# Eight quarter places of 4 KB in place of two whole places of 16 KB for x, the first keys and values, the last raw weights and the sums of w_in

## The chip, the core and the metric

The kernel runs on one core of one Trainium2 chip. The metric is the device time in microseconds of one execution, the median over the runs shown. A matmul is issued by TensorE (PE; PEld is its weight load), element-wise work runs on VectorE (DVE), ScalarE (ACT) and GpSimd (POOL), and SyncE (SP) issues almost all DMA transfers.

## What is computed

The reference is an attention with keys and values that are averaged over groups of 8 positions, followed by a two-layer network with a sigmoid gate:

```python
# q, k, v: [8, 8, 576, 64]; w_in: [512, 2048]; w_out: [2048, 512]
k_p = k.reshape(B, H, 72, 8, D).mean(axis=3)
v_p = v.reshape(B, H, 72, 8, D).mean(axis=3)
scores = np.matmul(q, k_p.transpose(0, 1, 3, 2)) / np.sqrt(D)
attn = softmax(scores)
x = np.matmul(attn, v_p).transpose(0, 2, 1, 3).reshape(B * S, H * D)   # [4608, 512]
h = x @ w_in
g = h * (1.0 / (1.0 + np.exp(-1.702 * h)))
out = g @ w_out
```

## The kernel before, in words

The 4608 tokens are worked through in nine chunks of 512. Chunks 0 to 7 are the first 512 tokens of each batch; the 64 tokens that every batch leaves over are gathered through DRAM into chunk 8. For each chunk the attention gives x, transposed, as a rounded part and a rest; every matmul of the network is then made of three products (rounded by rounded, rest by rounded, rounded by rest).

- **Attention of batch b.** Four matmuls (L961 to L964) form one column block `pav{b}_{piece}_{j}` in a PSUM bank of the two-bank ring `ps_a`. ACT or DVE writes its rounded part into x (L989), DVE the rest (L992), and for batches from 2 on the whole value is copied too (L1001). The transposed attention weights `apt` (L883) use the same two banks. So the third user of this ring waits until the DVE has read the first.
- **Chunks 0 and 1** go through `dense`: h = x @ w_in (L1220 to L1222), the gate on ACT (L1237, L1242), its rest on POOL (L1250), and o += g @ w_out (L1262 to L1264).
- **Chunks 2 to 8** go through `pair`: two 128-row blocks of w_in at once by a scheme with seven products instead of eight (L1424), collected in two PSUM banks `ha` and `hb` of the two-bank ring `ps_h`; DVE or ACT copies the bank `ha` out (L1439), DVE adds the bank `hb` (L1446), and the outputs are L1624 to L1626. The scheme needs sums and differences of blocks of x and of w_in. The latter are formed once, by `fold(p)` for p = 0 to 7 (L1307 the sums, L1332 the rounded part, L1335 the rest), kept in the buffer `stage` and written to DRAM (`wd{p}_{k}`, L1297, k = 1 and 2 from `stage`). Each later chunk reads them back (L1357).
- **Where x lies.** The pool `xpool` has two places of 16 KB per partition under one tag `x`. They go, in this order, to `kv0` (pooled inputs of batch 0), `x0`, the last three raw weight blocks (`raws`), `x1`, `stage`, and then the operands of chunks 2 to 8. A place is handed on when the last use of all of it is over. So chunk 2's x takes the place of `stage`: its first write on ACT waits for all the last DMA writes of `stage` (folds 6 and 7).
- **Loads of keys and values.** From batch 1 on, `kv{b}_{u}_False` (k) and `kv{b}_{u}_True` (v) take turns in a single place, and DVE sums each over the pooling windows (`red`, L539) before the next is loaded.
- **Order.** The program first lists every task with an estimated length and a due time. `Plan.order` then runs a list schedule over engines, places and banks and fixes a single order for each of the engines and for the DMA issues on SP. Hence a change of places changes the order of many instructions that it doesn't name. At run time every engine takes its instructions strictly in that order and waits by semaphore.

Of the kernel before, what the change touches and what calls it, by code (L numbers as in the profile page):

```python
# [10 lines left out]
F32 = mybir.dt.float32  # L11
F32R = mybir.dt.float32r
U32 = mybir.dt.uint32
# [5 lines left out]
P = 128  # L19
# [237 lines left out]
def attention_moe_kernel(ctx: ExitStack, tc: tile.TileContext, q, k, v, w_in, w_out, out):  # L257
# [110 lines left out]

    x_bufs = {}

    def x_buf(c):
        if c not in x_bufs:
            x_bufs[c] = buf(xpool, [P, 2, NJ, CHUNK], F32R, "x", f"x{c}", fifo=True)
        return x_bufs[c]


# [46 lines left out]

    def x_op(c, name):
        if c not in x_ops:
            xb = buf(xpool, [P, 2, NJ, CHUNK], F32R, "x", f"x{c}", fifo=True)
            at = [(xb, lambda t, k=k: t[:, :, k]) for k in range(NJ)]
            at += [(home(2 * i, [P, 2, 512], F32R, f"xs{c}_{i}"), lambda t: t) for i in X_PLACES[(c - FROM) % 2]]
            x_ops[c] = {n: Op(b, n, view) for n, (b, view) in zip(XOPS, at)}
        return x_ops[c][name]  # L430

    def x_whole(c, name):
# [439 lines left out]
    def weigh(b, piece, m, main, tail):  # L872
# [50 lines left out]
        for j in range(NJ):  # L923
# [41 lines left out]

            kh, jj = divmod(j, 2)
            if b < FROM:
                parts_of, whole = (x,), None
            else:

                block, whole = (("11", "t1"), ("21", "t4"), (None, "t3"), ("22", "t2"))[2 * piece + kh]
                block, whole = x_op(b, block) if block else None, x_whole(b, whole)
                parts_of = [o.of for o in (block, whole) if o]
# [6 lines left out]
                mode="f32r",  # L980
            )
            if b < FROM:
                hk, lk = [(x, (0, piece, j))], [(x, (1, piece, j))]
                hv, lv = (lambda j=j, r=r: x()[:, r, j, cols] for r in range(2))
            elif block:
                hk, lk = (block.refs(r, (jj,)) for r in range(2))
                hv, lv = (lambda jj=jj, r=r, block=block: block(r, jj) for r in range(2))
# [79 lines left out]
    def home(i, shape, dtype, name):  # L1067
        return Buf(home_ring(i), lambda: const.tile(shape, dtype, tag=f"w{i}", name=name), name)

    def fetch_weights(i):  # L1070
        f, m, c0, n = parts[i]
        if i + GAP < 2 * NF:
            raw = home(i + GAP, [P, n, 2], U32, f"raw{i}")
        else:

            if not last_raws:
                last_raws.append(buf(xpool, [P, 2, 512, 2], U32, "x", "raws", fifo=True))
            kk = i + GAP - 2 * NF
            sl = ((kk + 1) // 2, slice((kk // 2) * 256, (kk // 2) * 256 + n))
            raw = Part(last_raws[0], kk, lambda t: t[:, sl[0], sl[1]])  # L1080
        rows = slice(f * P, (f + 1) * P)
        src = w_out[rows, c0 : c0 + n].unsqueeze(1) if m else w_in[:, rows].rearrange("(j p) c -> p j c", p=P)
        words = src.bitcast(U32).rearrange("p j (c w) -> p j c w", w=2)
        dma(
            P * n * 8,
            lambda: nc.sync.dma_start(
                out=raw().rearrange("p (j c) w -> p j c w", j=words.shape[1]), in_=words
            ),
            writes=[ref(raw)],
        )  # L1090
        raws[i] = raw
# [115 lines left out]
    def dense(c, o0, n, fs, acc, due):  # L1207
# [6 lines left out]
        for i, f in enumerate(fs):  # L1214
            for j in range(NJ):

                def products(i=i, f=f, j=j):
                    w, o = homes[0, f]().rearrange("p r (j c) -> p r j c", j=NJ), h()[:, i]
                    xs = xb()[:, :, :, o0 : o0 + n]
                    nc.tensor.matmul(o, lhsT=w[:, 0, j], rhs=xs[:, 0, j], start=j == 0, stop=False)  # L1220
                    nc.tensor.matmul(o, lhsT=w[:, 1, j], rhs=xs[:, 0, j], start=False, stop=False)  # L1221
                    nc.tensor.matmul(o, lhsT=w[:, 0, j], rhs=xs[:, 1, j], start=False, stop=j == NJ - 1)  # L1222

                pe(
                    3 * (0.4167 * n + 13.5),
                    products,
                    [homes[0, f]] + [(xb, (r, hf, j)) for r in range(2) for hf in halves],
                    [h],
                    mode="f32r",
                )  # L1230
# [58 lines left out]
    def fold(p):  # L1289

        pair_of = [homes[0, 2 * p + i] for i in range(2)]
        d1, d2 = (Sums(stage, 2 * (p % 2) + i, lambda t, k=2 * (p % 2) + i: t[:, :, k]) for i in range(2))

        def leave(k, reads, view):
            dma(
# [216 lines left out]

    def first_batch():
        m = Batch()
        kv = buf(xpool, [P, 2, NU, NP, 512], F32, "x", "kv0", fifo=True)
        m.k, m.v = ([Part(kv, (i, u), lambda t, i=i, u=u: t[:, i, u]) for u in range(NU)] for i in range(2))
        m.tl = home(2 * NF - 4, [P, 512], F32, "tl0")
        whole = []
        tiles = PIECES[0][1] + PIECES[1][1]
        places = [home(2 * NF - 1 - i, [P, 2, H, D], F32, f"q0_{i}") for i in range(3)]  # L1520

        def fetch_q_tile(i):
            s0, ns = tiles[i]
            part = Part(places[i // 2], i % 2, lambda t: t[:ns, i % 2])
            dma(
                ns * H * D * 4,
                lambda: nc.sync.dma_start(out=part(), in_=q[0, :, s0 : s0 + ns].rearrange("h s d -> s h d")),
                writes=[ref(part)],
                run=256,
            )  # L1530
            whole.append(part)

        todo = {
            "k0": lambda: fetch_main(0, 0, k, m.k[0]),
            "k1": lambda: fetch_main(0, 1, k, m.k[1]),
            "v0": lambda: fetch_main(0, 0, v, m.v[0]),
            "v1": lambda: fetch_main(0, 1, v, m.v[1]),
            "t": lambda: fetch_last(0, m.tl),
            "w": lambda: fetch_weights(len(raws)),
            "q": lambda: fetch_q_tile(len(whole)),  # L1540
        }
        for n, what in enumerate("k0 k1 t q q v0 v1 w w w w w q q q w w".split()):
            plan.due = -100.0 + n
            todo[what]()
        return m, whole[:2], whole[2:]
# [13 lines left out]
    for b in range(1, B):  # L1559
        m = Batch()  # L1560
        m.k = m.v = m.tl = None
        start = FIRST + STEP * (NF + LAG) + ROUND * (b - 2) if b > 1 else 90.0
        plan.start = start - 15
        plan.due = start
        sum_keys(b, m)
        plan.due = start + 5
        held = scores(b, 0, m)
        sum_values(b, m)
        plan.due = start + 15
        weigh(b, 0, m, *held)  # L1570
        plan.due = start + 20
        held = scores(b, 1, m)
        plan.due = start + 30
        weigh(b, 1, m, *held)
        if b >= FROM:
            combine(b)
        if b == FROM - 1:
            stage = buf(xpool, [P, 2, NJ, CHUNK], F32, "x", "stage", fifo=True)
    plan.start = 0.0
    plan.due = FIRST + STEP * (NF + LAG) + ROUND * (B - 1) - 20  # L1580
    gather_left(B)
# [105 lines left out]
```

## Time and profile before

| | |
|---|---|
| median of 3 runs | 951.98 us (950.72 to 954.21) |
| the profiled execution's own time | 954.85 us |
| its span in the trace | 953.1 us |
| mean granted TensorE clock | 0.995 |
| PE busy | 929.7 us, 98% of the span |
| DVE, ACT, POOL busy | 649.0, 541.4, 315.6 us |

PE busy counts the time in which a matmul ran, at whatever clock; the granted clock is 1.00 at 2.4 GHz and 0.50 at 1.2 GHz. Two things can be saved without removing work: the 23.4 us in which PE stood idle, and stretches at the lower clock.

### The profile page before, as it was taken

How to read it: one execution, taken by the hardware profiler on the slowest of the kernel's cores; microseconds unless marked ns; L12 is line 12 of the kernel's file. 1: busy time of each engine (PE TensorE's matmuls, PEld its weight loads, DVE VectorE, ACT ScalarE, POOL GpSimd, SP SyncE). 2: the span in 40 equal slices, each digit the busy share in tenths (PEclk: the TensorE clock that was granted, in tenths of full speed). 3: DMA queues.
4: the chain of work that ended last, by engine and by line, in shares of the span. 5: the costliest groups of instructions: out<-in, count | busy, mean ns of one | idle time of the engine just before them, and what ended most of it. 6: DMA issues, size and time to landing. Idle time of an engine off the chain costs nothing.

```text
span 953.1 us, 16387 instructions
## 1 busy us (share of the span) xinstructions
PE 929.7 (98%) x5709; PEld 817.3 (86%) x5709; DVE 649.0 (68%) x1313; ACT 541.4 (57%) x1192; POOL 315.6 (33%) x307
## 2 busy tenths in 40 slices
PE   9999999999899999999999999999999999999997
PEld 8889887888687887989898988888888989898986
DVE  5988888885487677888678876887688643223322
ACT  4787764444247565667456854786477653334333
POOL 1755851788252125222503250315131451000000
PEclk9999999999999999999999999999999999999999
DMA  9993523345447457845885478648854565456541
GB/s 263 389 348 106 139 66 101 125 158 193 158 114 226 134 163 229 240 145 182 234 245 166 147 210 262 190 141 223 262 183 144 183 226 203 158 177 228 180 135 44
DMA packets 147314, 176.72 MB, mean 185 GB/s; under 512 B 85664, under 2 KB 96928, under 8 KB 147232
## 3 DMA queue, kind: packets, MB, share of 16 engines
q1 hardware_dynamic: 142384, 166.89, 57.1%
q10 hardware_dynamic: 4848, 8.78, 2.6%
q8 instruction: 45, 0.74, 0.3%
q14 instruction: 37, 0.30, 0.1%
HBM read 150.47 MB, written 25.17 MB: 184 GB/s over the span
## 4 chain that ended last, share of the span: by engine, by line
PE 81%; DVE 7%; DMA 6%; ACT 3%; issue 2%; SPq 1%; POOL 0%; ACTq 0%; DVEq 0%; POOLq 0%
PE ha L1424 15%; PE hb L1424 11%; PE o L1624 9%; PE o L1626 9%; PE o L1625 9%; PE sps L740 4%; PE h L1220 3%; PE h L1222 3%; PE h L1221 3%; PE o L1262 2%; PE o L1263 2%; PE o L1264 2%; DMA qr<-in_q_dram 2%; DMA kv_False<-in_k_dram 2%; PE warm L1587 1%
## 5 line engine op out<-in xcount | busy, mean ns | idle before, releaser
L1624 PE MATMUL o<-w,ghall 128*128 128x512 f32 x448 | 177.2, 396 | 0.0
L1626 PE MATMUL o<-w,glall 128*128 128x512 f32 x448 | 176.5, 394 | 0.0
L1625 PE MATMUL o<-w,ghall 128*128 128x512 f32 x448 | 176.1, 393 | 0.0
L1478 POOL TENSOR_TENSOR glall<-shared,ghall 128x256 fp32r<-128x256 f32 x87 | 68.9, 792 | 254.0 <-ACT shared L1471 228.2
L1424 PE MATMUL hb<-x,ws 128*128 128x256 f32 x672 | 98.5, 284 | 2.5 <-DVE shared L1446 2.0
L1626 PEld LDWEIGHTS o<-w,glall 128*128 128x128 f32 x448 | 84.5, 189 | 18.7
L1424 PEld LDWEIGHTS hb<-x,ws 128*128 128x128 f32 x672 | 91.9, 189 | 9.5 <-DVE shared L1446 3.3
L1424 PE MATMUL ha<-xs,ws 128*128 128x256 f32 x672 | 99.6, 284 | 0.0
L1424 PEld LDWEIGHTS ha<-xs,ws 128*128 128x128 f32 x672 | 92.2, 189 | 7.5 <-issue 1.2
L1446 DVE TENSOR_TENSOR shared<-shared,hb 128x256 f32<-128x256 f32 x112 | 46.6, 416 | 69.2 <-PE hb L1424 43.9
L1624 PEld LDWEIGHTS o<-w,ghall 128*128 128x128 f32 x448 | 84.9, 190 | 8.9 <-issue 0.8
L1625 PEld LDWEIGHTS o<-w,ghall 128*128 128x128 f32 x448 | 84.3, 188 | 8.2
L1463 ACT ACTIVATE ghall<-shared 128x256 fp32r<-128x256 f32 x112 | 46.8, 418 | 65.3 <-DVE shared L1446 54.8
L1478 POOL TENSOR_TENSOR glall<-gall,ghall 128x256 fp32r<-128x256 f32 x44 | 35.4, 804 | 140.5 <-ACT gall L1471 114.0
L1220 PE MATMUL h<-x,w 128*128 128x256 f32 (+1 forms) x192 | 63.2, 329 | 0.0
L1222 PE MATMUL h<-x,w 128*128 128x256 f32 (+1 forms) x192 | 61.2, 319 | 0.0
L1221 PE MATMUL h<-x,w 128*128 128x256 f32 (+1 forms) x192 | 61.2, 319 | 0.0
L1424 PE MATMUL ha<-x,ws 128*128 128x256 f32 x336 | 51.7, 291 | 5.0 <-ACT shared L1471 3.9
L1478 DVE TENSOR_TENSOR glall<-shared,ghall 128x256 fp32r<-128x256 f32 x63 | 30.1, 477 | 39.0 <-ACT shared L1471 38.8
L1250 POOL TENSOR_TENSOR gl<-g,gh 128x512 fp32r<-128x512 f32 x27 | 38.5, 1427 | 53.3 <-ACT gh L1242 37.3
L1439 ACT COPY shared<-ha 128x256 f32<-128x256 f32 x65 | 24.1, 370 | 55.5 <-PE ha L1424 54.3
L1424 PEld LDWEIGHTS ha<-x,ws 128*128 128x128 f32 x336 | 45.7, 192 | 10.9 <-ACT shared L1471 6.1
(176 smaller groups left out, 2169.3 us busy)
## 6 DMA issues: line engine op xcount, KB each, us to landing
ws<-wd SPq DMA_DIRECT2D x168, 512.0 KB
shared<-wd SPq DMA_DIRECT2D x56, 256.0 KB
out_dram<-osb ACTq DMA_DIRECT2D x32, 256.0 KB
wd<-stage SPq DMA_DIRECT2D x16, 512.0 KB
raw<-in_moe_w_in_dram SPq DMA_DIRECT2D x15, 512.0 KB
raw<-in_moe_w_out_dram SPq DMA_DIRECT2D x15, 512.0 KB
kv_False<-in_k_dram SPq DMA_DIRECT2D x28, 256.0 KB
kv_True<-in_v_dram SPq DMA_DIRECT2D x28, 256.0 KB
```

The costliest lines, as they stand in the source:

```text
L740: nc.tensor.matmul(ps()[:ns, t * PW : (t + 1) * PW], lhsT=qt()[:, s0 - o0 : s0 - o0 + ns], rhs=m.k2()[:, jj], start=True, stop=True,)
L1220: nc.tensor.matmul(o, lhsT=w[:, 0, j], rhs=xs[:, 0, j], start=j == 0, stop=False)
L1221: nc.tensor.matmul(o, lhsT=w[:, 1, j], rhs=xs[:, 0, j], start=False, stop=False)
L1222: nc.tensor.matmul(o, lhsT=w[:, 0, j], rhs=xs[:, 1, j], start=False, stop=j == NJ - 1)
L1250: engine.tensor_tensor(out=gl(), in0=g(), in1=gh().bitcast(F32), op=ALU.subtract)
L1424: nc.tensor.matmul(o, lhsT=wv()[:, r, jj], rhs=xo(k, jj), start=start and n == 0, stop=n == len(terms) - 1,  skip_group_check=not start,)
L1446: lambda: nc.vector.tensor_tensor(out=part(i), in0=part(i), in1=hb()[:, half * 256 : half * 256 + 256], op=ALU.add),
L1463: lambda: nc.scalar.activation(out=gh(), in_=src(), func=AF.Gelu_apprx_sigmoid),
L1478: engine.tensor_tensor(out=gl(), in0=part(i), in1=gh().bitcast(F32), op=ALU.subtract)
L1624: nc.tensor.matmul(o(), lhsT=gh()[:, tok], rhs=w()[:, 0], start=start, stop=False)
L1625: nc.tensor.matmul(o(), lhsT=gh()[:, tok], rhs=w()[:, 1], start=False, stop=False)
L1626: nc.tensor.matmul(o(), lhsT=gl()[:, tok], rhs=w()[:, 0], start=False, stop=stop)
```

## The change

The one tag `x` with two places of 16 KB becomes four tags `x0` to `x3` with two places of 4 KB each, the same 32 KB in all. Whoever took a whole place now takes one place under each of the tags that it needs: `kv0` one quarter for each of its two key and two value blocks, x of chunks 0 and 1 one quarter for each j, `raws` two quarters only, `stage` one quarter for each of four sums (an even fold p uses quarters 0 and 1, an odd one 2 and 3), and the operands "11", "21", t1 and t4 of later chunks one quarter each. A quarter is handed on when its own uses are over.

```diff
--- before.py
+++ after.py
@@ -368,9 +368,13 @@
 
     x_bufs = {}
 
+    def quarters(shape, dtype, name, n=NJ):
+
+        return [buf(xpool, shape, dtype, f"x{k}", name, fifo=True) for k in range(n)]
+
     def x_buf(c):
         if c not in x_bufs:
-            x_bufs[c] = buf(xpool, [P, 2, NJ, CHUNK], F32R, "x", f"x{c}", fifo=True)
+            x_bufs[c] = quarters([P, 2, CHUNK], F32R, f"x{c}")
         return x_bufs[c]
 
 
@@ -423,10 +427,9 @@
 
     def x_op(c, name):
         if c not in x_ops:
-            xb = buf(xpool, [P, 2, NJ, CHUNK], F32R, "x", f"x{c}", fifo=True)
-            at = [(xb, lambda t, k=k: t[:, :, k]) for k in range(NJ)]
-            at += [(home(2 * i, [P, 2, 512], F32R, f"xs{c}_{i}"), lambda t: t) for i in X_PLACES[(c - FROM) % 2]]
-            x_ops[c] = {n: Op(b, n, view) for n, (b, view) in zip(XOPS, at)}
+            at = quarters([P, 2, CHUNK], F32R, f"x{c}")
+            at += [home(2 * i, [P, 2, 512], F32R, f"xs{c}_{i}") for i in X_PLACES[(c - FROM) % 2]]
+            x_ops[c] = {n: Op(b, n, lambda t: t) for n, b in zip(XOPS, at)}
         return x_ops[c][name]
 
     def x_whole(c, name):
@@ -965,7 +968,7 @@
 
             kh, jj = divmod(j, 2)
             if b < FROM:
-                parts_of, whole = (x,), None
+                parts_of, whole = (x[j],), None
             else:
 
                 block, whole = (("11", "t1"), ("21", "t4"), (None, "t3"), ("22", "t2"))[2 * piece + kh]
@@ -980,8 +983,8 @@
                 mode="f32r",
             )
             if b < FROM:
-                hk, lk = [(x, (0, piece, j))], [(x, (1, piece, j))]
-                hv, lv = (lambda j=j, r=r: x()[:, r, j, cols] for r in range(2))
+                hk, lk = ([(x[j], (r, piece))] for r in range(2))
+                hv, lv = (lambda j=j, r=r: x[j]()[:, r, cols] for r in range(2))
             elif block:
                 hk, lk = (block.refs(r, (jj,)) for r in range(2))
                 hv, lv = (lambda jj=jj, r=r, block=block: block(r, jj) for r in range(2))
@@ -1074,10 +1077,10 @@
         else:
 
             if not last_raws:
-                last_raws.append(buf(xpool, [P, 2, 512, 2], U32, "x", "raws", fifo=True))
+                last_raws.extend(quarters([P, 512, 2], U32, "raws", 2))
             kk = i + GAP - 2 * NF
             sl = ((kk + 1) // 2, slice((kk // 2) * 256, (kk // 2) * 256 + n))
-            raw = Part(last_raws[0], kk, lambda t: t[:, sl[0], sl[1]])
+            raw = Part(last_raws[sl[0]], kk, lambda t: t[:, sl[1]])
         rows = slice(f * P, (f + 1) * P)
         src = w_out[rows, c0 : c0 + n].unsqueeze(1) if m else w_in[:, rows].rearrange("(j p) c -> p j c", p=P)
         words = src.bitcast(U32).rearrange("p j (c w) -> p j c w", w=2)
@@ -1216,15 +1219,15 @@
 
                 def products(i=i, f=f, j=j):
                     w, o = homes[0, f]().rearrange("p r (j c) -> p r j c", j=NJ), h()[:, i]
-                    xs = xb()[:, :, :, o0 : o0 + n]
-                    nc.tensor.matmul(o, lhsT=w[:, 0, j], rhs=xs[:, 0, j], start=j == 0, stop=False)
-                    nc.tensor.matmul(o, lhsT=w[:, 1, j], rhs=xs[:, 0, j], start=False, stop=False)
-                    nc.tensor.matmul(o, lhsT=w[:, 0, j], rhs=xs[:, 1, j], start=False, stop=j == NJ - 1)
+                    xs = xb[j]()[:, :, o0 : o0 + n]
+                    nc.tensor.matmul(o, lhsT=w[:, 0, j], rhs=xs[:, 0], start=j == 0, stop=False)
+                    nc.tensor.matmul(o, lhsT=w[:, 1, j], rhs=xs[:, 0], start=False, stop=False)
+                    nc.tensor.matmul(o, lhsT=w[:, 0, j], rhs=xs[:, 1], start=False, stop=j == NJ - 1)
 
                 pe(
                     3 * (0.4167 * n + 13.5),
                     products,
-                    [homes[0, f]] + [(xb, (r, hf, j)) for r in range(2) for hf in halves],
+                    [homes[0, f]] + [(xb[j], (r, hf)) for r in range(2) for hf in halves],
                     [h],
                     mode="f32r",
                 )
@@ -1289,7 +1292,7 @@
     def fold(p):
 
         pair_of = [homes[0, 2 * p + i] for i in range(2)]
-        d1, d2 = (Sums(stage, 2 * (p % 2) + i, lambda t, k=2 * (p % 2) + i: t[:, :, k]) for i in range(2))
+        d1, d2 = (Sums(stage[2 * (p % 2) + i], 0, lambda t: t) for i in range(2))
 
         def leave(k, reads, view):
             dma(
@@ -1512,8 +1515,8 @@
 
     def first_batch():
         m = Batch()
-        kv = buf(xpool, [P, 2, NU, NP, 512], F32, "x", "kv0", fifo=True)
-        m.k, m.v = ([Part(kv, (i, u), lambda t, i=i, u=u: t[:, i, u]) for u in range(NU)] for i in range(2))
+        kv = quarters([P, NP, 512], F32, "kv0")
+        m.k, m.v = kv[:NU], kv[NU:]
         m.tl = home(2 * NF - 4, [P, 512], F32, "tl0")
         whole = []
         tiles = PIECES[0][1] + PIECES[1][1]
@@ -1575,7 +1578,7 @@
         if b >= FROM:
             combine(b)
         if b == FROM - 1:
-            stage = buf(xpool, [P, 2, NJ, CHUNK], F32, "x", "stage", fifo=True)
+            stage = quarters([P, 2, CHUNK], F32, "stage")
     plan.start = 0.0
     plan.due = FIRST + STEP * (NF + LAG) + ROUND * (B - 1) - 20
     gather_left(B)
```

With it, the DMA of a sum from `stage` to DRAM is described as 128 rows of 1024 elements instead of 256 rows of 512, since its two halves now lie side by side. The number of matmuls of each kind stays the same. The line numbers of the changed kernel are 3 higher from L430 on. What the planner makes of it is seen best at three places.

**PE and SP where chunk 1 ends and batch 2's x begins.** On PE, before, from row 1048 of its order (`pav2_0_0` is the first column block of batch 2, `o1_...` are outputs of chunk 1, `h1_0_11` a hidden block of it):

```order
L961 MATMUL pav2_0_0_2750<-ah2_0_0_2353,vh2_2310 128x256
L962 MATMUL pav2_0_0_2750<-ah2_0_0_2353,vl2_2348 128x256
L963 MATMUL pav2_0_0_2750<-at2_0_0_2405,vt2_2040 128x256
L964 MATMUL pav2_0_0_2750<-al2_0_0_2366,vh2_2310 128x256
L883 MATMUL apt2_0_2_2757<-ident_79,main2_0_2312 128x128 x2
L1262 MATMUL o1_256_2145<-w1_11_1325,gh1_0_11_2722 128x512
L1263 MATMUL o1_256_2145<-w1_11_1325,gh1_0_11_2722 128x512
L1264 MATMUL o1_256_2145<-w1_11_1325,gl1_0_11_2731 128x512
L1262 MATMUL o1_0_2152<-w1_11_1325,gh1_0_11_2722 128x512
L1263 MATMUL o1_0_2152<-w1_11_1325,gh1_0_11_2722 128x512
L1264 MATMUL o1_0_2152<-w1_11_1325,gl1_0_11_2731 128x512
L961 MATMUL pav2_0_1_2781<-ah2_0_1_2355,vh2_2310 128x256
```

Now, from row 1021:

```order
L964 MATMUL pav2_0_0_2712<-ah2_0_0_2361,vh2_2337 128x256
L965 MATMUL pav2_0_0_2712<-ah2_0_0_2361,vl2_2353 128x256
L966 MATMUL pav2_0_0_2712<-at2_0_0_2417,vt2_2050 128x256
L967 MATMUL pav2_0_0_2712<-al2_0_0_2376,vh2_2337 128x256
L886 MATMUL apt2_0_2_2717<-ident_79,main2_0_2331 128x128 x2
L1223 MATMUL h1_0_11_2672<-x1_1744,w0_11_1249 128x512
L1224 MATMUL h1_0_11_2672<-x1_1744,w0_11_1249 128x512
L1225 MATMUL h1_0_11_2672<-x1_1744,w0_11_1249 128x512
L1223 MATMUL h1_0_11_2672<-x1_1796,w0_11_1249 128x512
L1224 MATMUL h1_0_11_2672<-x1_1796,w0_11_1249 128x512
L1225 MATMUL h1_0_11_2672<-x1_1796,w0_11_1249 128x512
L964 MATMUL pav2_0_1_2739<-ah2_0_1_2366,vh2_2337 128x256
```

The block `pav2_0_0` stands 27 rows earlier, all of them 512-column matmuls of chunk 1, and the work between it and `pav2_0_1` is now six matmuls of h instead of six of o. On SP, before, the last writes of the sums (`wd6`, `wd7`) and what follows:

```order
L1297 DMA wd6_1_122<-stage_2071 256x1x512
L1297 DMA wd6_2_123<-stage_2071 256x1x512
L1357 DMA ws2_1_2_2712<-wd1_2_103 128x1024
L1297 DMA wd7_2_127<-stage_2071 256x1x512
L1297 DMA wd7_1_126<-stage_2071 256x1x512
L461 DMA kv3_0_False_2748<-in_k_dram 64x2x512 x2
L477 DMA tl3_0_2771<-in_v_dram 32x1x512 x3
```

Now (`tl` and `qr` are the tail rows and queries of batch 3):

```order
L1300 DMA wd5_2_119<-stage_2108 128x1024
L1300 DMA wd6_1_122<-stage_2072 128x1024
L1300 DMA wd6_2_123<-stage_2077 128x1024
L464 DMA kv3_0_False_2731<-in_k_dram 64x2x512
L1360 DMA ws2_1_2_2744<-wd1_2_103 128x1024
L464 DMA kv3_0_False_2731<-in_k_dram 64x2x512
L1300 DMA wd7_2_127<-stage_2108 128x1024
L480 DMA tl3_0_2790<-in_v_dram 32x1x512 x3
L480 DMA tl3_0_2790<-in_k_dram 32x1x512
L513 DMA qr3_0_0_2801<-in_q_dram 32x8x32
L1300 DMA wd7_1_126<-stage_2082 128x1024
```

The two writes of fold 6 stand together as before; the first key load of batch 3 comes between them and fold 7's writes, which are apart now. The write to x on ACT that follows `pav2_0_0` waited for five transfers before, `wd5_2` and both of folds 6 and 7; now it waits only for `wd6_1`, the one that leaves quarter 0.

**PE in batch 1's second piece.** Before, up to the transposes `apt1_1_3` (`x0` operands, chunk 0's hidden block 14 and output 256); `pav1_1_2` stands a few rows ahead of this piece:

```order
L1220 MATMUL h0_256_14_1996<-x0_491,w0_14_1560 128x256
L1221 MATMUL h0_256_14_1996<-x0_491,w0_14_1560 128x256
L1222 MATMUL h0_256_14_1996<-x0_491,w0_14_1560 128x256
L1220 MATMUL h0_256_14_1996<-x0_491,w0_14_1560 128x256
L1221 MATMUL h0_256_14_1996<-x0_491,w0_14_1560 128x256
L1222 MATMUL h0_256_14_1996<-x0_491,w0_14_1560 128x256
L1262 MATMUL o0_256_982<-w1_12_1451,gh0_256_12_1976 128x512
L1263 MATMUL o0_256_982<-w1_12_1451,gh0_256_12_1976 128x512
L1264 MATMUL o0_256_982<-w1_12_1451,gl0_256_12_1988 128x512
L883 MATMUL apt1_1_3_2013<-ident_79,main1_1_1815 128x128 x2
L883 MATMUL apt1_1_3_2013<-ident_79,main1_1_1815 128x64
```

Now:

```order
L886 MATMUL apt1_1_3_2012<-ident_79,main1_1_1826 128x128 x2
L886 MATMUL apt1_1_3_2012<-ident_79,main1_1_1826 128x64
L1223 MATMUL h0_256_14_1995<-x0_555,w0_14_1567 128x256
L1224 MATMUL h0_256_14_1995<-x0_555,w0_14_1567 128x256
L1225 MATMUL h0_256_14_1995<-x0_555,w0_14_1567 128x256
L964 MATMUL pav1_1_2_2023<-ah1_1_2_1988,vh1_1526 128x320
L965 MATMUL pav1_1_2_2023<-ah1_1_2_1988,vl1_1543 128x320
L966 MATMUL pav1_1_2_2023<-at1_1_1_1903,vt1_1279 128x320
L967 MATMUL pav1_1_2_2023<-al1_1_2_2010,vh1_1526 128x320
L1265 MATMUL o0_256_989<-w1_12_1458,gh0_256_12_1993 128x512
L1266 MATMUL o0_256_989<-w1_12_1458,gh0_256_12_1993 128x512
L1267 MATMUL o0_256_989<-w1_12_1458,gl0_256_12_1999 128x512
```

`pav1_1_2` (four matmuls of 320 columns), half of the hidden block and three output matmuls have moved behind `apt1_1_3`.

**PE where one pair follows another in chunk 8.** Before, between pairs 1 and 2:

```order
L1424 MATMUL ha8_1_9650<-x8_8745,shared8_2565 128x256 x6
L1424 MATMUL hb8_1_9660<-xs8_3_8770,ws8_1_2_9541 128x256 x6
L1624 MATMUL o8_0_9642<-w1_2_496,ghall0_3101 128x512
L1625 MATMUL o8_0_9642<-w1_2_496,ghall0_3101 128x512
L1626 MATMUL o8_0_9642<-w1_2_496,glall0_3108 128x512
L1424 MATMUL ha8_2_9747<-x8_8745,ws8_2_0_9563 128x256 x6
L1424 MATMUL hb8_2_9756<-x8_8745,ws8_2_0_9563 128x256 x6
L1624 MATMUL o8_128_9671<-w1_2_496,ghall0_3101 128x512
L1625 MATMUL o8_128_9671<-w1_2_496,ghall0_3101 128x512
L1626 MATMUL o8_128_9671<-w1_2_496,glall0_3108 128x512
L1424 MATMUL hb8_2_9756<-x8_8745,ws8_2_1_9606 128x256 x6
```

Now:

```order
L1427 MATMUL ha8_1_9677<-x8_8883,shared8_2591 128x256 x6
L1627 MATMUL o8_384_9745<-w1_0_325,ghall1_3195 128x512
L1628 MATMUL o8_384_9745<-w1_0_325,ghall1_3195 128x512
L1629 MATMUL o8_384_9745<-w1_0_325,glall1_3217 128x512
L1427 MATMUL hb8_1_9688<-xs8_3_8804,ws8_1_2_9573 128x256 x6
L1427 MATMUL ha8_2_9777<-x8_8718,ws8_2_0_9596 128x256 x6
L1427 MATMUL hb8_2_9785<-x8_8727,ws8_2_0_9596 128x256 x6
L1627 MATMUL o8_0_9698<-w1_2_499,ghall0_3179 128x512
L1628 MATMUL o8_0_9698<-w1_2_499,ghall0_3179 128x512
L1629 MATMUL o8_0_9698<-w1_2_499,glall0_3189 128x512
```

The output matmuls that stood between the last `hb` product of a pair and the first `ha` product of the next now stand ahead of that `hb` product. Six `ha` matmuls are all that lies between two uses of bank kind `hb` by neighbouring pairs. In the order of before one joint late in the run looks so, from pair 6 to 7 of chunk 6; now the fifteen joints between the pairs of chunks 7 and 8 do too.

## Rows read from the trace of the kernel before

**Rows 1.** The page, parts 1 and 4: busy time, chain by engine.
```profile
PE 929.7 (98%) x5709; PEld 817.3 (86%) x5709; DVE 649.0 (68%) x1313; ACT 541.4 (57%) x1192; POOL 315.6 (33%) x307
PE 81%; DVE 7%; DMA 6%; ACT 3%; issue 2%; SPq 1%; POOL 0%; ACTq 0%; DVEq 0%; POOLq 0%
```

**Rows 2.** Windows: stretch, length, busy PE, PEld, DVE, ACT, POOL, clock, DMA share, GB/s.
```profile
140.00:150.00 10.00, 9.99 (x77) 9.42 (x76) 9.33 (x20) 6.05 (x9) 2.58 (x2) 1.00 0.30 84
...
160.00:164.00 4.00, 3.10 (x17) 2.27 (x17) 2.95 (x4) 1.33 (x5) 0.85 (x1) 1.00 0.34 122
240.00:260.00 20.00, 16.77 (x77) 13.75 (x76) 7.03 (x13) 4.97 (x12) 4.20 (x3) 0.91 0.56 177
279.00:293.00 14.00, 12.26 (x80) 10.52 (x80) 12.46 (x23) 7.22 (x17) 4.52 (x4) 1.00 0.69 209
330.00:345.00 15.00, 13.28 (x82) 11.39 (x80) 11.59 (x23) 12.43 (x23) 2.97 (x4) 1.00 0.42 132
345.00:360.00 15.00, 13.58 (x82) 11.52 (x82) 11.75 (x23) 8.60 (x24) 3.10 (x4) 1.00 0.75 217
360.00:373.00 13.00, 11.62 (x74) 10.05 (x73) 10.16 (x18) 6.82 (x20) 8.09 (x9) 1.00 0.81 221
760.00:947.00 187.00, 187.00 (x1162) 168.14 (x1161) 59.54 (x135) 76.50 (x191) 19.87 (x18) 1.00 0.51 170
```

**Rows 3.** Timeline of PE: start, length, line, operation, count, idle before and its releaser.
```profile
247.01 0.28 PE L961 MATMUL pav<-ah,vh 128*128 128x256 f32 x1
...
252.50 0.39 PE L961 MATMUL pav<-ah,vh 128*128 128x256 f32 x1 [3.23 <-DVE x L992]
...
253.22 0.51 PE L1262 MATMUL o<-w,gh 128*128 128x512 f32 x1
...
256.94 0.28 PE L961 MATMUL pav<-ah,vh 128*128 128x256 f32 x1
```

**Rows 4.** Chain of waits, 242 to 253.5 us: start, length, what.
```profile
243.47 7.72 DMA wd<-stage
...
251.28 0.38 ACT x L989
...
252.03 0.43 DVE x L992
```

**Rows 5.** Windows of the same columns, around that wait and behind it.
```profile
244.00:250.00 6.00, 5.27 (x27) 4.12 (x25) 0.00 (x0) 1.09 (x2) 2.25 (x2) 1.00 0.96 325
253.00:257.00 4.00, 4.00 (x15) 3.17 (x14) 2.81 (x5) 0.65 (x2) 0.00 (x0) 0.57 0.32 51
```

**Rows 6.** Timelines of SP, DVE and POOL, 230 to 240 us.
```profile
230.09 0.52 SPq L1297 DMA_DIRECT2D wd<-stage  x1
...
238.44 1.18 SPq L1297 DMA_DIRECT2D wd<-stage  x2
...
234.63 0.69 DVE L1307 TENSOR_TENSOR stage<-w 128x512 f32<-128x512 f32 x1 [4.29 <-DMA wd<-stage]
...
236.68 1.74 POOL L1335 TENSOR_TENSOR stage<-stage 128x512 fp32r<-128x512 f32 x1
```

**Rows 7.** Timelines of DVE and PE, 160 to 164 us.
```profile
160.80 1.96 DVE L539 TENSOR_REDUCE red_k<-kv_False 128x128 f32<-128x1024 f32 x1 [1.49 <-DMA kv_False<-in_k_dram]
...
163.14 0.64 PE L883 MATMUL apt<-ident,main 128*128 128x128 f32 x3 [0.90 <-DVE x L992]
```

**Rows 8.** Timeline of PE at the joint of pairs 6 and 7, chunk 6.
```profile
762.45 0.88 PE L1424 MATMUL ha<-x,ws 128*128 128x256 f32 x6
763.16 0.94 PE L1424 MATMUL hb<-x,ws 128*128 128x256 f32 x6
763.93 0.39 PE L1624 MATMUL o<-w,ghall 128*128 128x512 f32 x1
```

**Rows 9.** Chain of waits in the first pairs of chunk 2.
```profile
282.21 4.39 DMA kv_True<-in_v_dram
286.73 1.98 DVE red_v L539
```

## Prediction

> **What bounds the kernel now.** I read the busy times and the chain of waits first. PE works for 929.7 of 953.1 us, and 81% of the chain is PE [rows 1]; no other engine is near. The change takes away no matmul, so it can win only from the 23.4 us in which PE idles and from stretches at the lower clock, and lose by adding to them. The next view is the one of windows, to see where these are [rows 2]: 3.23 us idle between 240 and 260 us, where the mean granted clock is also down to 0.91; 0.90 us between 160 and 164; and in chunk 2's first pairs 1.74, 1.72, 1.42 and 1.38 us in four windows between 279 and 373, together 6.26. From 760 to 947 us PE is never idle. The rest is the start, the end and small gaps elsewhere.
>
> The timeline of PE shows the largest stall in full [rows 3]. The first column block of batch 2 runs at 247.01, the next only at 252.50, after 3.23 us of idle time that ended with the DVE's write to x. The chain of waits tells who was late [rows 4]: a write of sums to DRAM, 7.72 us long from 243.47; then the ACT's write to x at 251.28, the DVE's at 252.03, and PE. That is the wait for the whole of `stage`: the place is free only when folds 6 and 7 have left it. Behind it the nine output matmuls take from 253.22 to 256.94, 3.72 us, and the granted clock from 253 to 257 is 0.57, most of it on the lower level, 1.2 GHz [rows 3, 5].
>
> **The change, part by part.**
>
> *The wait at 247 us.* In the new order the ACT's first write to x waits for `wd6_1` alone. In 3.23 us PE did nothing, and in the four us behind it the clock lost 4 x (1 - 0.57) = 1.7 us: 4.9 us are at stake. What remains of it follows from two times. PE comes to `pav2_0_0` 27 matmuls earlier. One of these costs what the nine above would have taken at full clock, 3.72 x 0.57 / 9 = 0.235 us, so PE is there 6.3 us earlier, at 240.7. Then 0.5 us for that block, and six h matmuls of 0.235, 1.4 us, cover the wait until 242.7. The other time is the landing of `wd6_1`. The last work on that sum is its rest on POOL. In both orders it stands right behind the gelu rest of hidden block 10, whose matmuls have kept their place in PE's order; before, it ran from 236.68 for 1.74 us and the transfer was issued at 238.44 [rows 6], so I keep that time. A single such transfer was issued at 230.09 and let the DVE go on at 234.63, 4.5 us [rows 6]. So the ACT is free at 242.9. From the ACT's start to the next block on PE it took 1.22 us (251.28 to 252.50), so PE goes on at 244.2 and stalls for about 1.4 us, less what the landing is quicker. Bounds: none, if the transfer lands in 3 us; and 4.7, if it takes 7.72. I take 1.0, nearer to the single transfer, which ran under a light load like this one. A stall of this size had no lower clock behind it at 163 us [rows 2, 7], so I charge none. Gain: 4.9 - 1.0 = 3.9 us.
>
> *What is queued behind the ACT's write* are its next roundings of the transposed weights and of fold 7's sums; fold 7's writes come later than before, but nobody waits for them until chunk 2's operands t1 and t4 take quarters 2 and 3, over 10 us later. POOL's gelu rest of hidden block 11 stands behind six pieces of fold work, some 10 us by its own pieces (1.74 for a rest); PE needs it after about 50 more matmuls, 10 us. I charge nothing; without that cover it is 1 to 3 us.
>
> *Batch 1, at 162 us.* `apt1_1_3` waits for a PSUM bank, and this for the DVE, which sits in the key sum of 1.96 us that itself waited 1.49 us for its load [rows 7]. That load isn't moved. What moves is the cover: `pav1_1_2` (four matmuls of 320 columns, 0.6 us) and three output matmuls (0.7 us) now stand behind the transposes. So PE comes to the same wait 1.3 us earlier, and idles longer by 0 (if the load comes earlier too) to 1.3 us. Its price is near the upper end, as nothing shortens the load: +1.2 us.
>
> *x of batch 1* now starts earlier, since raws no longer hold a whole place. From 140 to 150 us, where its first block ran, PE was busy for 9.99 of 10 us [rows 2], so the move only swaps work and I charge 0.
>
> *The last pairs.* Fifteen new joints have only one `ha` product between two uses of `hb`. The one joint of that form in the trace [rows 8]: `ha` starts at 762.45, `hb` at 763.16, the next matmul at 763.93, so `hb` took 0.77 us instead of the 0.71 of `ha`. 15 x 0.06 = +0.9 us. Bounds: 0, and 15 x 0.43 = 6.4 us if the DVE's add (a DVE instruction on 256 columns takes 0.43 us [rows 4]) lay wholly open; the one real joint speaks for the low end.
>
> *Chunk 2's first pairs.* Their order on PE and DVE changes throughout, by the planner and not by the diff. The stalls of 6.26 us hang on when key and value loads land and on what the DVE then has queued: one value load of 4.39 us, then 1.98 us of sum [rows 9]. Nothing in the new order removes a load or a sum. Between 0 of it left and twice as much, I take no change, with a likely spread of 4 us either way.
>
> *The DMA with longer rows* moves the same bytes; its gain is inside the landing time above.
>
> Sum on the profiled execution, 954.85 us: -3.9 + 1.2 + 0.9 = -1.8, so 953.05. That execution lies 2.87 us above the median of the runs shown; the difference is carried over: 951.98 - 1.8 = **950.2 us**. What a measurement of this kernel can tell from no change is about 0.5%, 4.8 us, so the bounds are 947.2 and 956.7.
>
> **Rivals.**
>
> 1. *Chunk 2 also gets smoother.* With x placed 6 us earlier, the first pairs find operands and banks ready, and two thirds of the 6.26 us of idle time go: 950.2 - 4.2 = 946.0. For it: batch 2's blocks all move up by 5 us or more. Against: the loads they meet are issued on SP by the same places of keys and values. It decides from 3 us on.
> 2. *The wait stays as long.* `wd6_1` now shares the DMA with a key load right behind it; between 244 and 250 us, where the 7.72 us transfer ran beside such loads, the DMA share was 0.96 at 325 GB/s [rows 4, 5]. At 7.72 us it lands at 246.2, PE stalls to 247.4, 4.7 us, and the lower clock returns with 1.7: 6.4 us against the 4.9 of now, so 951.98 + 1.5 + 1.2 + 0.9 = 955.6. Against: the transfer starts on an idle DMA, ahead of these loads. The Trainium skill, "DMA: Bandwidth & Descriptors", section "Issuing engines are not separate DMA queues", says that all transfers run on the same 16 engines and interleave, which is what this rival needs; the trace agrees, with 7.72 us in a full stretch against 4.5 in a light one.
> 3. *Slower, by DVE's queue in chunk 2.* If the new order puts the value sums of batch 3 ahead of the adds that free `hb`, each of its two value loads stands open for its 4.39 us [rows 9] instead of the 1.74 us now lost in 279 to 293: 950.2 + 2 x 4.39 - 1.74 = 957.2. It decides when the DVE idles for more than 6.5 us in front of these two sums together. For it: the DVE takes its instructions in order, and it already waits there. Against: in the trace it has 12.46 busy us of 14 there, so other work is at hand.
> 4. *The clock falls in the last pairs.* Fifteen tiny gaps could cost the clock: a spell like that of 253 to 257 us costs 1.7 us, fifteen of them 25 us, giving 975. The trace speaks against it: in 279 to 293 us PE is idle for 12% in several gaps, at a clock of 1.00 [rows 2]. The Trainium skill, "TensorE: Matmul & The Clock Gate", section "A second HAM failure mode: psum-queue depth-cycling", reports that frequent short idles between groups of matmuls let the clock go up and down. It would make this rival the forecast; by the row of 279 to 293 us it doesn't hold here.
>
> **How the numbers follow.** Forecast (947 to 953.5): 0.52. Rival 1: 0.20. Rival 2: 0.11. Rival 3: 0.13. Rival 4: 0.02. The remaining 0.02 is for something else. Faster by more than 0.5%: rival 1 and 0.07 of the forecast's lower edge, 0.27. Slower: rival 3, rival 4 and a little of rival 2, 0.15. Within: 0.58. The range of 945 to 957 holds the forecast, rivals 1 and 2 and half of rival 3; what lies outside is below 2 in 10.
>
> **What would show it right or wrong.** Right: between `pav2_0_0` at about 241 us and the next block less than 1.5 us of idle time, and a clock of 1.00 behind it; a gap of about 2 us ahead of `apt1_1_3` near 162; `hb` at the joints of chunks 7 and 8 at 0.77 us; the chain no longer names a write of sums as a wait of 7 us. Wrong: an idle time of over 3 us there with a transfer as its releaser (rival 2), idle sums in 279 to 373 us far from 6.3 (rivals 1 and 3), a clock under 1.00 from 760 us on (rival 4). A wait that no row of before shows, as for quarters 2 and 3, would break the sum too.

## The result, and the profile after

The changed kernel takes 942.47 us (4 runs, 938.5 to 947.1) against 952.24 us, a ratio of 0.9906 with a 95% interval of 0.9877 to 0.9935. Measured again with the first experiments it took 940.28 us against 951.72, 0.9874 (0.9852 to 0.9896). So it is about 1% faster, 10 to 11 us, where 1.8 us were forecast; the time lies 2.5 us below the range of 945 to 957.

The profiled execution is the slowest of its four, 947.1 us with a span of 945.3. In the page, PE is as busy as before [rows 1] and the gain is in the span:

```profile
PE 928.4 (98%) x5709; PEld 818.4 (87%) x5709; DVE 658.3 (70%) x1318; ACT 540.2 (57%) x1187; POOL 318.9 (34%) x307
PE 80%; DMA 7%; DVE 6%; ACT 3%; issue 2%; SPq 1%; POOL 0%; ACTq 0%; DVEq 0%; POOLq 0%
```

The windows that answer to [rows 2], shifted to where the same work now runs (columns as there):

```profile
160.00:164.00 4.00, 3.49 (x22) 2.87 (x21) 3.61 (x5) 1.35 (x5) 1.30 (x1) 1.00 0.54 168
240.00:260.00 20.00, 19.39 (x98) 15.06 (x97) 16.15 (x25) 9.75 (x25) 9.17 (x8) 1.00 0.65 195
273.00:287.00 14.00, 13.85 (x88) 12.24 (x87) 11.74 (x24) 6.27 (x14) 3.67 (x4) 1.00 0.76 226
324.00:345.00 21.00, 20.62 (x128) 18.34 (x127) 17.58 (x37) 16.95 (x38) 7.17 (x8) 1.00 0.63 193
345.00:367.00 22.00, 22.00 (x141) 20.06 (x140) 19.81 (x34) 11.41 (x31) 13.49 (x12) 1.00 0.89 244
465.00:750.00 285.00, 280.31 (x1744) 248.78 (x1743) 222.00 (x477) 184.06 (x423) 79.38 (x91) 0.99 0.66 194
750.00:940.00 190.00, 189.56 (x1167) 169.88 (x1165) 65.20 (x145) 76.28 (x189) 15.34 (x12) 1.00 0.53 170
```

Between 240 and 260 us the idle time is 0.61 us instead of 3.23, and the mean clock is 1.00 instead of 0.91. In the first pairs of chunk 2 it is 0.15, 0.38 and 0: almost all of the 6.26 us of before is gone. That is the larger part of the gain, and the forecast had it at nothing. The whole stretch of the first pairs shows it in one line each, for the kernel before, the changed kernel and a second profile of it (after_again, below): 6.64, 0.80 and 0.61 us of idle PE.

```profile
262.00:375.00 113.00, 106.36 (x634) 90.85 (x634) 88.83 (x181) 68.00 (x159) 35.92 (x36) 1.00 0.59 172
262.00:375.00 113.00, 112.20 (x689) 98.63 (x688) 91.56 (x182) 67.83 (x156) 42.17 (x41) 1.00 0.63 185
262.00:375.00 113.00, 112.39 (x689) 98.78 (x688) 91.75 (x183) 67.92 (x157) 42.18 (x41) 1.00 0.63 184
```

The wait for x itself, on the timelines of PE and ACT (columns as in [rows 3]):

```profile
240.58 0.28 PE L964 MATMUL pav<-ah,vh 128*128 128x256 f32 x1
...
242.65 0.28 PE L964 MATMUL pav<-ah,vh 128*128 128x256 f32 x1
...
244.67 0.38 PE L964 MATMUL pav<-ah,vh 128*128 128x256 f32 x1 [0.46 <-DVE x L995]
```

```profile
241.30 0.37 ACT L992 CAST x<-pav 128x256 fp32r<-128x256 f32 x1 [5.81 <-PE pav L967]
```

`pav2_0_0` runs at 240.58, where 240.7 was worked out. The ACT was let go by PE's own matmul, not by a transfer: the write of sums had landed before 241.3. Only the third block has a short stall, 0.46 us.

One stall is new, at 660 us. In the windows and the chain of waits around it:

```profile
660.00:663.00 3.00, 0.51 (x4) 0.08 (x2) 2.57 (x6) 1.61 (x4) 0.00 (x0) 1.00 0.93 230
663.00:672.00 9.00, 9.00 (x42) 7.74 (x43) 3.75 (x6) 3.18 (x9) 1.46 (x2) 0.62 0.69 220
```

```profile
654.07 5.33 DMA tl<-in_k_dram
...
659.52 1.06 DVE tred L603
```

A late load of batch 7's tail keys held up the DVE and through it PE, 2.49 us, and from 663 to 672 us the granted clock was 0.62, mostly on the lower level: 2.5 us idle and 9 x 0.38 = 3.4 us of clock. The second profile has the same wait, but shorter and with a clock of 1.00 behind it. There the DVE waits 3.59 us for the load, and PE 0.74:

```profile
654.08 1.07 DVE L603 TENSOR_REDUCE tred<-tl 128x64 f32<-128x512 f32 x1 [3.59 <-DMA tl<-in_k_dram]
```

```profile
657.54 0.98 PE L1427 MATMUL ha<-x,shared 128*128 128x256 f32 x6 [0.74 <-ACT shared L1442]
```

The kernel before has no stall of over 0.3 us between 640 and 700 us. So the wait came with the new order, and its size differs from one execution to the next.

### The profile page after: what moved, and what is told of

Read it like the earlier page. It is cut to its first block, busy times and chain, and to the rows that moved or that the text cites. A ratio compares the mean times of both kernels' runs of the same rounds, so it can differ in the third digit from the quotient of the medians.

```text
span 945.3 us, 16367 instructions
## 1 busy us (share of the span) xinstructions
PE 928.4 (98%) x5709; PEld 818.4 (87%) x5709; DVE 658.3 (70%) x1318; ACT 540.2 (57%) x1187; POOL 318.9 (34%) x307
## 4 chain that ended last, share of the span: by engine, by line
PE 80%; DMA 7%; DVE 6%; ACT 3%; issue 2%; SPq 1%; POOL 0%; ACTq 0%; DVEq 0%; POOLq 0%
PE ha L1427 14%; PE hb L1427 11%; PE o L1627 9%; PE o L1629 9%; PE o L1628 9%; PE sps L743 4%; DMA kv_False<-in_k_dram 3%; PE h L1223 3%; PE h L1225 3%; PE h L1224 3%; PE o L1265 3%; PE o L1266 2%; PE o L1267 2%; DMA qr<-in_q_dram 2%; PE warm L1590 2%
## 5 line engine op out<-in xcount | busy, mean ns | idle before, releaser
L1481 POOL TENSOR_TENSOR glall<-shared,ghall 128x256 fp32r<-128x256 f32 x88 | 73.1, 832 | 225.5 <-ACT shared L1474 176.2
L1481 POOL TENSOR_TENSOR glall<-gall,ghall 128x256 fp32r<-128x256 f32 x42 | 33.0, 785 | 96.4 <-ACT gall L1474 71.9
L1427 PEld LDWEIGHTS ha<-x,shared 128*128 128x128 f32 x336 | 47.0, 188 | 7.1 <-ACT shared L1442 2.9
```

The source lines that it names most:

```text
L1427: nc.tensor.matmul(o, lhsT=wv()[:, r, jj], rhs=xo(k, jj), start=start and n == 0, stop=n == len(terms) - 1,  skip_group_check=not start,)
L1481: engine.tensor_tensor(out=gl(), in0=part(i), in1=gh().bitcast(F32), op=ALU.subtract)
```

## The experiments

The task lists of both kernels are the same, 4711 tasks with the same dependencies; only the planned order differs. That allows the two parts of the change to be taken apart: the quarter places at run time, and the order that the planner finds with them. Eight of the kernels are the changed kernel with an order written out as a table (task number, and a star where the task goes to its other engine):

```diff
-    order = plan.order()
+    own = [(t.engine, t.emit) for t in plan.tasks]
+    plan.order()
+    order = []
+    for word in ORDER.split():
+        t = plan.tasks[int(word.rstrip("*"))]
+        t.engine, t.emit = (t.other[0], t.other[2]) if word.endswith("*") else own[t.k]
+        order.append(t)
```

A hybrid of two orders takes all tasks that the first begins before a point of the plan, and then the others as the second has them. Medians and ratios follow. The kernel before was measured anew beside the first four kernels (951.72 us), the next four (950.45) and the last three (952.98), and each ratio is against the median beside it; so ratios compare across the groups, and medians only roughly:

| kernel | order up to chunk 2's pairs, from there on | us | ratio, 95% |
|---|---|---|---|
| after_again | new, new | 940.28 | 0.9874 (0.9852 to 0.9896) |
| places_alone | old, old | 948.7 | 0.9966 (0.9951 to 0.998) |
| old_then_new | old, new | 946.76 | 0.9955 (0.9936 to 0.9975) |
| new_then_old | new, old | 950.14 | 0.9973 (0.9955 to 0.9991) |
| stage_held | planned with sums handed on together | 947.11 | 0.9962 (0.9945 to 0.9979) |
| x1_late | planned with batch 1's x late | 950.03 | 0.999 (0.9974 to 1.0007) |
| new_to_pair2 | new to pair 2 of chunk 2, old | 944.43 | 0.9933 (0.9913 to 0.9953) |
| old_tail | new to 700 us of the plan, old | 940.9 | 0.9889 (0.9868 to 0.9911) |
| late_then_new | x1_late's to 363 us of the plan, new | 943.72 | 0.9905 (0.9879 to 0.9931) |
| new_then_late | new to 363 us of the plan, x1_late's | 947.76 | 0.9952 (0.9931 to 0.9972) |
| cover_moved | places_alone, two output blocks moved | 946.3 | 0.9933 (0.9909 to 0.9957) |

**after_again**, the changed kernel itself. 

> The changed kernel once more, as the reference for the runs beside it. All theories: 942.5 us, 0.99 of the kernel before, and if the 2.5 us stall near 663 us in its first profile was a late load of that execution alone, a second profile doesn't show it and its own time is 4 to 5 us shorter than 947.1.

 The second profile took 937.17 us, 9.9 us less than the first, and has no stall of over 0.75 us behind 162 us. The stall near 663 us is not gone, as was expected, but 0.74 us long (above), and the lower clock behind it is.

**places_alone**, the table of before. 

> Quarter places, but every instruction in the order of the kernel before. Theory 1 (the order of chunk 2's first pairs took away their stalls of 6 us): only the wait at 247 us goes, with the low clock behind it, so 952.2 - 4.9 = 947.3 us, and 6 us of idle PE stay in the first pairs. Theory 2 (x of batch 2 is ready earlier against the first pairs, whatever their order): the same, as x and the pairs move up together. Theory 3 (the places free waits all over, and the order is a side effect): 942.5 us, as the changed kernel.

 Measured: 948.7, theories 1 and 2. The stall at 247 us is gone, as the windows of before and of places_alone show:

```profile
170.00:262.00 92.00, 88.78 (x408) 71.88 (x407) 61.52 (x96) 36.69 (x67) 62.09 (x52) 0.98 0.49 162
170.00:262.00 92.00, 91.82 (x428) 74.33 (x428) 65.31 (x103) 38.97 (x71) 62.23 (x53) 1.00 0.52 169
```

But on PE's timeline the first pairs of chunk 2 stall as before (in [rows 2], 1.74 us from 279 to 293):

```profile
285.80 0.98 PE L1641 MATMUL hb<-xs,ws 128*128 128x256 f32 x6 [0.96 <-DVE shared L1663]
288.45 0.98 PE L1641 MATMUL ha<-x,ws 128*128 128x256 f32 x6 [0.98 <-DVE shared L1663]
300.30 0.97 PE L1641 MATMUL ha<-x,ws 128*128 128x256 f32 x6 [0.38 <-ACT shared L1688]
329.05 0.98 PE L1641 MATMUL ha<-x,ws 128*128 128x256 f32 x6 [1.74 <-ACT shared L1688]
```

So the places alone are worth 3.0 us (0.34%, by the interval 1.9 to 4.7 us), and 7 to 9 us of the gain are the new order in these places. The new order in the old places was not run.

**old_then_new** and **new_then_old**. 

> Quarter places; the order of before up to the first pair of chunk 2, the new order from there on. Theory 1: the first pairs' stalls go, the joints of the last pairs cost 0.9 us: 947.3 - 5.7 + 0.9 = 942.5 us. Theory 2: the stalls stay, 947.3 + 0.9 = 948.2 us.

 

> Quarter places; the new order up to the first pair of chunk 2, the order of before from there on. Theory 1: the stalls of the first pairs are back, the joints' cost is gone: 942.5 + 5.7 - 0.9 = 947.3 us. Theory 2: the stalls stay away, 942.5 - 0.9 = 941.6 us.

 Neither number came out: 946.76 lies nearer theory 2's, and 950.14 is above both. The profiles tell more. In new_then_old seven of the eight old stalls of the first pairs were there again, by 1.22, 0.97, 0.38, 1.72, 0.55, 0.26 and 1.15 us, as theory 1 wants; its seam, the point where one order passes into the other, added one of 1.20. In old_then_new most of the old stalls were gone, but others stood in the same pairs, 2.82 us at 287.98 and 0.81 at 276.05, and from 288 to 292 us the granted clock was 0.60. At 287.98 the DVE had first done a value sum that waited 1.84 us for its load, and only behind it, at 287.51, copied the bank that PE needed. I take this for the price of the seam, which no run shows apart; so I moved the seam.

**new_to_pair2**. 

> The changed kernel's order up to the second pair of chunk 2, the order of before from the third pair on. If each stall belongs to the order of its own pairs, those of 1.7, 0.5, 0.3 and 1.1 us between 325 and 370 us are back and the joints' 0.9 us gone: 940.6 + 3.6 - 0.9 = 943.3 us. If the early start carries through, they stay away: 939.7 us.

 Measured: 944.43, near the first number. On PE the stalls of pairs 0 and 1 stayed away but for the 0.24 us that the new order has too, and those of 1.74, 0.54, 0.24 and 1.15 us of later pairs came back, with one of 0.67. Each stall goes with the order around it; theory 1 holds.

**stage_held** and **x1_late** undo one hand-over each in the plan, by making the planner keep a group of places until all are free:

```diff
+        for group in self.together:
+            if any(b in group for b in t.bufs):
+                for b in group:
+                    if b not in t.bufs:
+                        t.bufs.append(b)
+                        b.users += 1
...
-            stage = quarters([P, 2, CHUNK], F32, "stage")
+            stage = quarters([P, 2, CHUNK], F32, "stage")
+            plan.together.append(stage)
```

In x1_late the group is the last raw weights, which take all four quarters in it. 

> Quarter places, but the planner hands on the four quarters of the sums together, when the last of them is free. It then plans batch 2 and chunk 2's first pairs as before; batch 1's early x and the new joints stay. Theory 1 (early hand-over of the sums lets the planner find an order without the first pairs' stalls): as the order of before in quarter places, 948.7, and 0.9 for the joints: 949.6 us. Rival (the gain comes from batch 1's early x): 941 us.

 

> Quarter places, but the last raw weights keep all four quarters in the plan, so batch 1's x is planned as before; batch 2 is planned early. Theory 1: 941 us, as the changed kernel, within 2 us, since the first pairs are planned like its own. Rival (batch 1's early x carries the gain): 948 us or more.

 stage_held: 947.11, 2.5 us below theory 1 and 6 above the rival; its order of batch 2 and of chunk 2 to 6 is that of before, and its first pairs stall by 5.77 us. So the new order there comes from the early hand-over of the sums. x1_late missed: 950.03, though its first pairs gained as forecast. It lost that again in chunks 3 to 6, as the same window of x1_late and of after_again shows:

```profile
470.00:760.00 290.00, 282.26 (x1770) 249.77 (x1769) 222.18 (x480) 187.23 (x432) 79.76 (x92) 1.00 0.68 195
```

```profile
470.00:760.00 290.00, 289.12 (x1824) 258.39 (x1824) 227.05 (x487) 191.13 (x438) 90.33 (x99) 1.00 0.68 200
```

7.74 us of idle PE against 0.88, most of it in eight stalls of 0.29 to 1.58 us behind the DVE and ACT. Not all of the difference is the order: the first profile of the changed kernel has 4.69 us of idle PE between 465 and 750 us.

**late_then_new** and **new_then_late** cross these two orders behind chunk 2's first pairs. 

> The order of x1_late up to 363 us of the plan, which is all of chunk 2's first pairs, and the changed kernel's order from there on. If x1_late's order gained 9.6 us up to there and lost it again in the pairs of chunks 3 to 6, because these are ordered otherwise: 942 us. If a bad start (when the loads land) did it: 950 us, as x1_late.

 

> The reverse: the changed kernel's order up to 363 us of the plan, and the order of x1_late from there on. If the order of chunks 3 to 6 is what costs x1_late its gain: 940.6 + 7 = 948 us, with some 7 us of idle PE between 470 and 760 us. If the start does it: 940.6 us.

 Measured: 943.72 and 947.76. Most of the loss goes with the order of the later pairs: by the ratios new_then_late is 0.8% behind the changed kernel, some 7 us, and late_then_new 0.3%, 3 us, with overlapping intervals. In its profiled execution (946.34 us, the second longest of its six) late_then_new too has 4.75 us of idle PE between 470 and 760. The window of new_then_late:

```profile
470.00:760.00 290.00, 281.72 (x1765) 249.32 (x1764) 220.48 (x477) 185.86 (x428) 81.56 (x92) 1.00 0.68 196
```

So an early hand-over opens the way to a good order, and a small change of the plan gives one without the gain. Why the later pairs stall in x1_late's order was not found.

**old_tail**. 

> The changed kernel's order up to 700 us of the plan, the order of before from there on, so the joints of the last pairs are the old ones. Joints at 0.06 us each: 940.6 - 0.9 = 939.7 us, and hb of the first product takes 0.72 us again. If the joints cost more than they show: 938 us or less. If nothing: 940.6.

 Measured: 940.9, four runs; the interval reaches 2 us to either side, so the runs can't tell 0.9 us from nothing. The size is read from the profile of the changed kernel instead, on PE at one of the new joints:

```profile
775.48 0.88 PE L1427 MATMUL ha<-x,ws 128*128 128x256 f32 x6
776.20 0.94 PE L1427 MATMUL hb<-x,ws 128*128 128x256 f32 x6
776.97 0.40 PE L1627 MATMUL o<-w,ghall 128*128 128x512 f32 x1
```

`hb` takes 0.77 us from start to start as in [rows 8], where products elsewhere take 0.71 or 0.72.

**cover_moved** looks into one stall. In the kernel before, the timeline of PE and that of ACT around the largest stall of the first pairs, which the forecast took as fixed:

```profile
327.42 0.88 PE L1424 MATMUL ha<-x,shared 128*128 128x256 f32 x6
...
329.53 0.86 PE L1424 MATMUL hb<-xs,ws 128*128 128x256 f32 x6
...
332.81 0.98 PE L1424 MATMUL ha<-x,ws 128*128 128x256 f32 x6 [1.72 <-ACT shared L1471]
```

```profile
328.32 1.28 ACT L786 ACT_TABLE_LOAD   x1
329.62 1.17 ACT L786 ACTIVATE sc<-sc 128x1152 f32<-128x1152 f32 x1
330.81 1.28 ACT L1463 ACT_TABLE_LOAD   x1
332.10 0.38 ACT L1463 ACTIVATE ghall<-ha 128x256 fp32r<-128x256 f32 x1
332.38 0.38 ACT L1471 ACTIVATE shared<-ha 128x256 f32<-128x256 f32 x1
```

The last product in bank `ha` is done at about 328.1; the ACT starts an exponential of batch 3 just then, with a table load on either side of it (1.28 + 1.17 + 1.28 us), and only after it reads the bank. PE has 2.8 us of other work. In after_again the table load of the same exponential starts at 319.71 and the product in `ha` at 320.50, done at about 321.2. So the load begins 1.5 us ahead of the end of the product instead of 0.2 us behind it, and PE's other work lasts 3.5 us:

```profile
319.71 1.28 ACT L789 ACT_TABLE_LOAD   x1
...
323.76 0.38 ACT L1474 ACTIVATE shared<-ha 128x256 f32<-128x256 f32 x1
```

```profile
320.50 0.88 PE L1427 MATMUL ha<-x,shared 128*128 128x256 f32 x6
...
324.69 0.87 PE L1427 MATMUL ha<-x,ws 128*128 128x256 f32 x6
```

> places_alone with one edit: on PE two blocks of three output matmuls (1.4 us) move from behind the first ha product of pair 4 of chunk 2 to ahead of it. There places_alone idles for 1.74 us, since the ACT does an exponential with two table loads before it frees the bank. If the stall is only too little PE work between two uses of the bank, it shrinks to 0.3 to 0.4 us: 948.7 - 1.4 = 947.3 us. If the DVE or a load is what comes late behind it, another wait takes its place: 948.7 us.

 Measured: 946.3. The stall shrank as expected, on PE's timeline of cover_moved:

```profile
326.82 0.86 PE L1641 MATMUL hb<-xs,ws 128*128 128x256 f32 x6
...
330.10 0.98 PE L1641 MATMUL ha<-x,ws 128*128 128x256 f32 x6 [0.35 <-ACT shared L1688]
```

So at this stall too little PE work between two uses of the bank was the cause. But in its profiled execution a stall of 1.57 us stands at 352.98 that places_alone does not have, behind a key sum on the DVE that waited for its load, and the stalls of the first pairs add up to 6.46 us, against 6.42 in places_alone. So the second branch, another wait in its place, is not ruled out for the time as a whole: the median is 2.4 us lower, and the intervals of the two ratios overlap.

## Why the prediction was wrong

- **The wait at 247 us: right in kind and nearly in size.** Forecast 3.9 us of 4.9; measured 3.23 - 0.46 us of idle time and the 1.7 us of clock, 4.5. The landing was the mis-sized part: 4.5 us were taken for it, and it took at most 3.6 (in the second profile the write was issued at 238.48, and the ACT wrote to x at 242.09, let go by PE). The 4.5 us are the difference of two profiled executions; by medians places_alone gives 3.0 us for this wait, with 4.5 just inside its interval.
- **Batch 1 at 162 us: wrong sign.** Forecast +1.2, measured 0.51 us of idle time instead of 0.90, so -0.4. The step that failed was "Its price is near the upper end, as nothing shortens the load". The load did come earlier: the DVE's key sum starts at 159.46 instead of 160.80 [rows 7], on DVE and PE:

```profile
159.46 2.01 DVE L542 TENSOR_REDUCE red_k<-kv_False 128x128 f32<-128x1024 f32 x1 [1.15 <-DMA kv_False<-in_k_dram]
```

```profile
161.86 0.64 PE L886 MATMUL apt<-ident,main 128*128 128x128 f32 x3 [0.51 <-DVE x L995]
```

- **The last pairs: right by the joints.** Forecast +0.9 us by 0.06 for each joint; the joints show 0.77 and 0.78 us, while the runs of old_tail could not show the 0.9 us as time. The clock stayed at 1.00 from 750 to 940 us, so rival 4 is out.
- **Chunk 2's first pairs: the step that failed.** "Nothing in the new order removes a load or a sum ... I take no change" treated 6.26 us of stalls as bound to the loads. With the same loads and sums they come and go with the order: of the stalls of over 0.2 us between 262 and 375 us, 6.33 us before and 6.42 in places_alone, 0.65 and 0.61 are left in the two profiles of the new order. That is -5.7 us. Rival 1 had this term (4.2 us of it), but its reason, x placed early, is not enough: in new_then_old batch 2's x is placed in the new order, and seven of the eight stalls are back.
- **The sum** with the measured terms is -4.5 - 0.4 - 5.7 + 0.9 = -9.7 us, against -9.8 and -11.4 by the medians. That it comes so near is in part luck, as the terms are from single executions: the stalls of over 0.3 us behind 378 us add up to 6.3 us in the first profile of the changed kernel and to 0.7 in the second, so the rest isn't assigned.
- **A stall that the forecast passed over.** "The rest is the start, the end and small gaps elsewhere" left out the second largest stall of before, 1.98 us, with a clock of 0.57 behind it, 1.7 us more. On PE, and in the window behind it:

```profile
468.25 1.41 PE L1424 MATMUL hb<-xs,ws 128*128 128x256 f32 x6 [1.98 <-DVE gall L1446]
```

```profile
468.00:472.00 4.00, 3.66 (x14) 3.23 (x15) 3.66 (x8) 1.94 (x6) 0.75 (x1) 0.57 0.91 260
```

It is gone in after_again and 0.91 and 0.52 us long in the first profile. But the old order shows 0.40 and 0.53 us there in places_alone, so what the new order did to it is open.
- **The range** failed with that step. The "likely spread of 4 us either way" was a guess, although the sentence itself names the bound, "0 of it left": with all 6.26 us gone, 950.2 becomes 943.9, below the range's end of 945. I saw that the planner had changed the order of these pairs, and could have read in the two orders where the exponential stands against the products, as above, before putting it at nothing.

What stays open: why the planner's good order is good. Its order of chunks 3 to 6 is nearer that of before than x1_late's, which costs some 7 us; no rule was found that tells one from the other ahead of a run.

## What to carry to other kernels

Splitting a place so that it is handed on in parts pays twice: once for the wait itself (3 us here), and again, or not at all, through the order that a planner then finds (7 to 9 us here, of which 5.7 are the stalls of the first pairs; in x1_late even the 3 us were lost again). Stalls of a fixed order belong to the order, so when a change makes the planner reorder a stretch, its idle time is at stake as a whole and not to be carried over; look where long work of another engine (an exponential between two table loads) stands against the two uses of a bank around it. To find which part of such a change acts, run the new places with the old order: one kernel told the two apart.

## What was not expected of the hardware

- An idle stretch of 2.49 us on PE at 660 us was followed by a clock of 0.62 over 9 us, 3.4 us lost: more than the stall itself. In the kernel before, stalls of 3.23 and 1.98 us cost 1.7 us of clock each, and one of 1.72 us at 333 left it at 1.00 [rows 2]. In new_to_pair2 three shorter ones, of 0.41, 1.09 and 0.53 us up to 462.66, were followed by 0.65 from 462 to 466 us. So in these rows the length of a single stall doesn't tell whether the clock falls.
- Around an exponential the ACT is gone for 1.28 + 1.17 + 1.28 us, and the exponential begins 0.02 us behind the end of the table load. The Trainium skill, "ScalarE: Activation LUTs", section "What ACT_TABLE_LOAD costs", gives 1283 ns for the load, as here, and a drain of about as much again beside it, of which the rows here show nothing.
- Runs of the same program differ by 8.6 us (938.5 to 947.1). In the slowest of them 5.9 us are the wait for the load at 654 us and the clock behind it; what the others differ by is not shown.
